# Gated linear attention and two expert layers: column blocks in runs, one scan per step, float32 second products in the first units

## The chip, the cores and the metric

The kernel runs on one core of a Trainium2 chip, as one program. The metric is device time in microseconds (us), as the median of several executions; lower is better. The core has five engines with a queue of instructions each: PE (TensorE; its weight loads are shown apart as PEld), DVE (VectorE), ACT (ScalarE), POOL (GpSimd) and SP (SyncE, which here issues the DMAs).

## The reference

Three stages follow one another on 3072 tokens (4 sequences of 768, width 384 = 8 heads of 48):

```python
f = 1.0 / (1.0 + np.exp(-f_logit))
for t in range(S):
    state = f[:, :, t, :, None] * state + einsum('bhd,bhe->bhde', k[:, :, t], v[:, :, t])
    y[:, :, t] = einsum('bhd,bhde->bhe', q[:, :, t], state)
# x = y as (3072, 384)
x = ((x @ w_a) * (x @ w_b)) @ w_out            # 384 -> 1536 -> 384
p = domain_probs / (domain_probs.sum(-1, keepdims=True) + 1e-09)
for e in range(4):                             # 384 -> 1024 -> 384
    out += p[:, e:e + 1] * (np.maximum(x @ w1[e], 0.0) @ w2[e])
```

The weights of both expert layers and the result are wanted to float32 accuracy. Here the weights of the first layer arrive as 64-bit floats.

## The kernel before

**Phase A** holds the attention and the first expert layer. The attention is cut into 24 steps `s` (6 chunks of 128 time steps for each of the 4 sequences). A step's tiles hold 8 heads as 4 column groups `j` of 128 times, with the two heads of a group in partitions 0 to 47 and 64 to 111. For a step, `a_exp` (L188) computes u = 1 + exp(-f_logit), the exponential on ACT and the addition on DVE (L191). `a_scan` (L194) makes the running product R of u with one DVE scan for each of the four groups (L196); its second operand `cap` is a bound that is broadcast along the row. From step `EARLY` (8) on, a reciprocal for each group follows on DVE (L200). `a_hat` scales k by R (on POOL) and q by 1/R; for the first 8 steps this takes a chain of ACT, POOL and DVE instructions (L217 to L225), for the others fewer (L211 to L215). `a_trans` (L238), `a_scores` (L251) and `a_out` (L286, L294, L303) are the step's matrix products, all in float32; `a_out` also makes the new state, 64 wide, of which 48 columns hold a head (L331, L333), and writes the step's x, split into two parts.

Every product of the expert layers is taken from split operands: a number is rounded to the format float32r (`hi`) and the rest is kept (`lo`), and hi·hi, hi·lo and lo·hi are summed in PSUM, three matmuls of one pass instead of one in float32. `split` (L116) does the first part on ACT (L118) and the rest on POOL or DVE (L119). The work of the first layer is cut into *units* `u`: one block `i` of 512 tokens and one column block `f` of 128 of the 1536 columns (the first four units are 256 tokens wide). A unit takes two first products (`half`, L342, 9 matmuls each), their product `ab` on DVE (L457), the split of `ab` into `hl` and of the block of `w_out` into `wo`, and, one unit later, the second product (`outp`, L354, 9 matmuls). Up to `u` = 19 the `lo` parts are POOL's work, from `LATE` (20) on DVE's. The 64-bit weights are converted by seven instructions each (`to_f32`, L100 to L113), six of them on DVE.

`attn_to` and `conv_to` interleave the steps' operations and the conversions with the units; a scheduler then settles each engine's order. `busy` (L172) fills PE's early gaps with products of a tile of zeros, `junk`.

**Phase B** is the second expert layer: for each expert `e`, token block `n` (6 of 512) and column block `f` (8 of 128), `b1` makes one first product (L490, 9 matmuls of 512 columns), evacuated by ACT (L492) and DVE (L493) into a tile `h`, of which the pool `hp` holds three; `b2` is the second product (L508, 12 matmuls of 384 columns into the banks 4 to 7). The loop at L534 writes them alternately: `b1` of a column block, then `b2` of the one before. The weights of the next expert are loaded and split by `load_e` as tiles come free.

Of the kernel before, what the change touches and what calls it, by code (L numbers as in the profile page):

```python
# [8 lines left out]
F32 = mybir.dt.float32  # L9
F32R = mybir.dt.float32r  # L10
BF16 = mybir.dt.bfloat16
# [29 lines left out]
CA = 2  # L41
FRAC = 0.4
LATE = 20
LIMIT = float(2.0 ** 60)
# [6 lines left out]
def gla_moe_moe_kernel(ctx: ExitStack, tc, qkf, vv, wab, wout, w12, probs, gq, gv, gp, out):  # L51
# [20 lines left out]
    mask = const.tile([128, 128], F32, tag="mask", name="mask")  # L72
    cap = const.tile([128, 1], F32, tag="cap", name="cap")
    nc.vector.memset(cap, 2.0 * LIMIT)
    pr = const.tile([128, NSTEP, NE], F32, tag="pr", name="pr")
    prs = const.tile([128, NSTEP], F32, tag="prs", name="prs")
    flags = const.tile([128, NSTEP, 3], F32, tag="flags", name="flags")
    junk = const.tile([128, 512], BF16, tag="junk", name="junk")
    nc.vector.memset(junk, 0.0)
# [49 lines left out]
    def phase_a(actx):  # L129
# [37 lines left out]
        def busy(n):  # L167

            if n:
                b = bank("o")  # L170
                for _ in range(n):
                    nc.tensor.matmul(b, junk[:, :128], junk, start=True, stop=True)  # L172

# [14 lines left out]
        def a_exp(s):  # L188
            u = T[s]["f"]
            nc.scalar.activation(out=u, in_=u, func=AF.Exp, scale=-1.0)  # L190
            nc.vector.tensor_scalar(out=u, in0=u, scalar1=1.0, scalar2=None, op0=ALU.add)  # L191
            T[s]["R"] = slot("R")

        def a_scan(s, j):  # L194
            u, R = T[s]["f"], T[s]["R"]
            nc.vector.tensor_tensor_scan(  # L196
                out=R[:, j], data0=u[:, j], data1=cap.to_broadcast([128, C]), initial=1.0, op0=ALU.mult, op1=ALU.min
            )
            if s >= EARLY:
                nc.vector.reciprocal(out=u[:, j], in_=R[:, j])  # L200

# [73 lines left out]
        def a_out(s):  # L275
# [14 lines left out]
            if c:  # L290
                for j in range(4):
                    for h in range(2):
                        r = 64 * h
                        nc.tensor.matmul(  # L294
                            yps[r:r + 64, j * C:(j + 1) * C], st[r:r + D, j], q[r:r + D, j],
                            start=False, stop=True, skip_group_check=True,
                        )
            if not last:
                ups = bank("u")
                for j in range(4):  # L300
                    for h in range(2):
                        r = 64 * h
                        nc.tensor.matmul(  # L303
                            ups[r:r + 64, j * 64:(j + 1) * 64], kt[:, j, r:r + 64], v[:, 2 * j + h],
                            start=j == 0, stop=True, skip_group_check=True,
                        )
# [18 lines left out]
            if not last:  # L325
                new = at.tile([128, 4, 64], F32, tag="st", name="st", bufs=B + 1)
                uv = ups[:, :256].rearrange("p (j e) -> p j e", j=4)
                pe = t["pe"].to_broadcast([128, 4, 64])
                sign = 1.0 if s >= EARLY else -1.0
# [17 lines left out]
        def outp(i, o, n, f, fs, w, hl):  # L347
            if (i, fs[0]) not in x2ps:
                x2ps[i, fs[0]] = [bank("o") for _ in range(KC)]
            banks = x2ps[i, fs[0]]  # L350
            for m in range(KC):
                for q, (a, b) in enumerate(((0, 0), (0, 1), (1, 0))):

# [38 lines left out]
        def prep_ops(n):  # L392
            return [lambda: a_exp(n)] + [lambda j=j: a_scan(n, j) for j in range(4)] + [lambda: a_hat(n)]

# [47 lines left out]
        for u, (i, o, n, f, fs) in enumerate(units):  # L442
# [12 lines left out]
            pb = half(i, o, n, f, 1)  # L455
            ab = g.tile([128, n], F32, tag="ab", name="ab")
            nc.vector.tensor_tensor(out=ab, in0=pb, in1=a, op=ALU.mult)  # L457
            hl = g.tile([128, 2, n], F32R, tag="hl", name="hl", bufs=2)
            split(nc.vector if u >= LATE else nc.gpsimd, hl[:, 0], hl[:, 1], ab)
            w = g.tile([128, 2, DM], F32R, tag="wo", name="wo", bufs=2)  # L460
            split(nc.vector if u >= LATE else nc.gpsimd, w[:, 0], w[:, 1], wo_all[:, f])
            attn_to(goal)
# [8 lines left out]
    def phase_b(bctx):  # L471
        xb = bctx.enter_context(tc.tile_pool(name="xb", bufs=NBLK - 1))
        hp = bctx.enter_context(tc.tile_pool(name="hp", bufs=3))
        stg = bctx.enter_context(tc.tile_pool(name="stg", bufs=2))
# [57 lines left out]
        pend = [(0, f) for f in range(3, NF2)] + [(e, f) for e in range(1, NE) for f in range(NF2)]  # L532
        prev = None
        for e, n, f in [(e, n, f) for e in range(NE) for n in range(NBLK) for f in range(NF2)]:  # L534
            h = b1(e, n, f)
            if prev is not None:
                b2(*prev)
            prev = (e, n, f, h)
            if e == 0 and f == 4 and n + 2 < NBLK:
                x2_split(n + 2, xb, "x2", None)  # L540
            if pend and (e, n) == (0, 0):
                load_e(*pend.pop(0))
            elif pend and pend[0][0] == e + 1:

                m = pend[0][1]
                if (n > m and f == 4) if m < 2 else (n == NBLK - 1 and f >= m - 1):
                    load_e(*pend.pop(0))
        b2(*prev)

# [204 lines left out]
```

## Time and profile before

| | us |
|---|---|
| median of 3 executions (1445.41 to 1447.91) | 1446.5 |
| the profiled execution, its own time | 1444.91 |
| span of the profiled execution | 1443.2 |
| PE busy, share of the span | 1397.1, 97% |
| PE weight loads | 1194.9, 83% |
| DVE busy | 601.7, 42% |
| ACT busy | 388.3, 27% |
| POOL busy | 220.8, 15% |

The page gives the whole span; where the two phases lie, and which engine is full in each, is read from the table by windows. Phase A ends at about 632 us. In the trace a row of the timeline gives the start and the length of a group of instructions; matmuls overlap, so the pace of a sequence is read from start to start and not from the length of a row.

### The profile page before, as it was taken

What the parts mean: (1) busy time and instruction counts of PE and PEld (TensorE: products, weight loads), DVE (VectorE), ACT (ScalarE), POOL (GpSimd) and SP (SyncE); (2) the same over time, 40 slices, a digit from 0 to 9 for tenths busy, and PEclk for the clock granted to TensorE, in tenths of its full rate; (3) what the DMA queues carried; (4) which work ended last, traced back from release to release, by engine and by line L of the source; (5) the groups of instructions that cost most, each with busy time, mean ns of one, the idle gap of its engine ahead of it and who ended that gap; (6) DMA issues with size and microseconds to landing.
All of it is one profiled execution on the core that took longest, in us unless ns stands there. A gap on an engine that the chain in (4) does not pass through costs nothing.

```text
span 1443.2 us, 18215 instructions
## 1 busy us (share of the span) xinstructions
PE 1397.1 (97%) x7623; PEld 1194.9 (83%) x7623; DVE 601.7 (42%) x976; ACT 388.3 (27%) x701; POOL 220.8 (15%) x144
## 2 busy tenths in 40 slices
PE   8778899999999999999999999999999999999998
PEld 4556687778878778889999999999999999999997
DVE  7999835884573834532222222222222222222221
ACT  5454423433342323441111211111211112111111
POOL 4456451010010101350000310000300002000000
PEclk9899999999999999999999999999999999999999
DMA  6444201221130100210000110000200001000001
GB/s 247 137 152 130 74 0 31 76 88 34 42 95 1 57 28 11 61 38 0 1 1 0 56 33 1 0 1 1 88 1 0 1 0 44 1 22 23 22 33 36
DMA packets 28170, 60.29 MB, mean 42 GB/s; under 512 B 4016, under 2 KB 9392, under 8 KB 28080
## 3 DMA queue, kind: packets, MB, share of 16 engines
q1 hardware_dynamic: 28080, 59.05, 13.0%
q8 instruction: 62, 1.02, 0.3%
q14 instruction: 28, 0.23, 0.1%
HBM read 51.95 MB, written 4.72 MB: 39 GB/s over the span
## 4 chain that ended last, share of the span: by engine, by line
PE 77%; DVE 1%; ACT 0%; POOL 0%; issue 0%; DVEq 0%; POOLq 0%
PE bank L508 28%; PE bank L490 28%; PE bank L342 13%; PE bank L354 6%; PE bank L286 1%; PE bank L251 1%; PE bank L294 1%; PE bank L303 0%; PE bank L238 0%; DVE hl L119 0%; DVE f L200 0%; DVE acc L518 0%; POOL k L211 0%; DVE ss L267 0%; DVE ab L457 0%
## 5 line engine op out<-in xcount | busy, mean ns | idle before, releaser
L508 PE MATMUL bank<-w,h 128*128 128x384 f32 x2304 | 435.0, 337 | 0.0
L490 PE MATMUL bank<-x,w 128*128 128x512 f32 x1728 | 430.5, 393 | 0.0
L508 PEld LDWEIGHTS bank<-w,h 128*128 128x128 f32 x2304 | 409.7, 188 | 16.9
L490 PEld LDWEIGHTS bank<-x,w 128*128 128x128 f32 x1728 | 321.4, 188 | 58.6
L493 DVE SCALAR_TENSOR_TENSOR h<-bank,h 128x512 fp32r<-128x512 f32 x192 | 132.7, 691 | 541.1 <-ACT h L492 541.1
L342 PE MATMUL bank<-xT,w 128*128 128x512 f32 (+1 forms) x1332 | 322.4, 391 | 4.6 <-DVE ab L457 2.2
L342 PEld LDWEIGHTS bank<-xT,w 128*128 128x128 f32 x1332 | 245.7, 191 | 57.5 <-DVE ab L457 3.1
L492 ACT ACTIVATE h<-bank 128x512 fp32r<-128x512 f32 x192 | 115.0, 599 | 624.9 <-PE bank L490 624.9
L354 PE MATMUL bank<-hl,wo 128*128 128x512 f32 (+1 forms) x666 | 166.3, 392 | 4.7 <-POOL hl L119 3.2
L354 PEld LDWEIGHTS bank<-hl,wo 128*128 128x128 f32 x666 | 122.7, 190 | 32.6 <-POOL hl L119 4.3
L119 POOL TENSOR_TENSOR w<-raw,w 128x768 fp32r<-128x768 f32 x32 | 59.1, 1846 | 579.7 <-ACT w L118 577.7
L457 DVE TENSOR_TENSOR ab<-bank,a 128x512 f32<-128x512 f32 (+1 forms) x74 | 49.7, 671 | 143.2 <-PE bank L342 135.0
L118 ACT CAST hl<-ab 128x512 fp32r<-128x512 f32 (+1 forms) x74 | 45.0, 608 | 102.9 <-DVE ab L457 102.8
L453 ACT COPY a<-bank 128x512 f32<-128x512 f32 (+1 forms) x74 | 42.4, 574 | 95.0 <-PE bank L342 94.8
L518 DVE SCALAR_TENSOR_TENSOR acc<-bank,pr,acc 128x384 f32<-128x384 f32 x72 | 40.9, 609 | 58.9 <-PE bank L508 58.9
L119 DVE TENSOR_TENSOR hl<-ab,hl 128x512 fp32r<-128x512 f32 x54 | 50.6, 937 | 29.4 <-ACT hl L118 29.4
L211 POOL TENSOR_TENSOR k<-k,R 128x512 f32<-128x512 f32 x16 | 21.4, 1335 | 245.9 <-DVE R L196 171.0
L200 DVE RECIPROCAL f<-R 128x128 f32<-128x128 f32 x64 | 58.0, 925 | 0.0
L118 ACT CAST wo<-wo_all 128x384 fp32r<-128x384 f32 x74 | 38.1, 516 | 38.3 <-PE bank L354 37.8
L119 POOL TENSOR_TENSOR hl<-ab,hl 128x512 fp32r<-128x512 f32 (+1 forms) x20 | 34.7, 1737 | 51.2 <-ACT hl L118 51.1
L118 ACT CAST w<-raw 128x768 fp32r<-128x768 f32 x32 | 26.8, 838 | 48.4 <-PE bank L508 34.4
L119 DVE TENSOR_TENSOR wo<-wo_all,wo 128x384 fp32r<-128x384 f32 x54 | 31.9, 590 | 12.9 <-ACT wo L118 12.9
(101 smaller groups left out, 775.4 us busy)
## 6 DMA issues: line engine op xcount, KB each, us to landing
raw<-in_w_dram SPq DMA_DIRECT2D x32, 384.0 KB, 3.1
raw<-in_wab_dram SPq DMA_DIRECT2D x12, 768.0 KB, 4.4
f<-in_qkf_dram SPq DMA_DIRECT2D x20, 256.0 KB, 2.7
k<-in_qkf_dram SPq DMA_DIRECT2D x20, 256.0 KB, 2.7
q<-in_qkf_dram SPq DMA_DIRECT2D x20, 256.0 KB, 3.0
v<-in_v_dram SPq DMA_DIRECT2D x20, 256.0 KB, 3.5
raw<-in_wout_dram SPq DMA_DIRECT2D x6, 768.0 KB, 4.7
out_dram<-acc SPq DMA_DIRECT2D x24, 192.0 KB, 1.9
```

The lines of the kernel that those rows point to most:

```text
L118: nc.scalar.copy(out=hi, in_=x)
L119: engine.tensor_tensor(out=lo, in0=x, in1=hi.bitcast(F32), op=ALU.subtract)
L200: nc.vector.reciprocal(out=u[:, j], in_=R[:, j])
L342: nc.tensor.matmul(p, l, r, start=m == 0, stop=m == len(ops) - 1)
L354: nc.tensor.matmul(banks[m][:, o:o + n], w[:, a, m * 128:(m + 1) * 128], hl[:, b], start=f == fs[0] and q == 0 and o == 0, stop=f == fs[-1 ...
L453: nc.scalar.copy(out=a, in_=pa)
L457: nc.vector.tensor_tensor(out=ab, in0=pb, in1=a, op=ALU.mult)
L490: nc.tensor.matmul(p, l, r, start=i == 0, stop=i == len(ops) - 1)
L492: nc.scalar.activation(out=h[:, 0], in_=p, func=AF.Relu)
L493: nc.vector.scalar_tensor_tensor(out=h[:, 1], in0=p, scalar=0.0, in1=h[:, 0].bitcast(F32), op0=ALU.max, op1=ALU.subtract)
L508: nc.tensor.matmul(src, h[:, b, t * 128:(t + 1) * 128], w2[e, f][:, a], start=f == 0 and q == 0, stop=f == NF2 - 1 and q == 2,)
L518: nc.vector.scalar_tensor_tensor(out=dst, in0=src, scalar=p, in1=dst, op0=ALU.mult, op1=ALU.add)
```

## The change

Four edits, each at its own place:

- In phase B the column blocks are taken in runs: `b1` of all blocks of a run, then `b2` of all blocks of the run before. A run is 4 blocks in the token blocks 1 to 4, 2 blocks in token blocks 0 and 5, and (1, 1, 2, 2, 2) at the very start. The pool `hp` holds 7 tiles instead of 3. `load_e` of the next expert stands behind the `b2` that frees its tile.
- One scan of 512 elements makes all four groups' running products. It starts afresh at each group because `cap` is now a full tile whose first element of each group is set to u itself (a copy of 4 elements on ACT), so that the minimum of product and cap there is u. The addition of 1 moves from DVE to ACT.
- In the first 8 units (`WHOLE`) the second product is taken from unsplit float32 operands: 3 float32 matmuls in place of 9, and no split of `ab` and `w_out`.
- The states are 48 columns wide instead of 64: fewer moving columns in L303, fewer stationary ones in L294, and fewer elements in L331 and L333. The tile `junk` is smaller and is read by broadcast; its matmuls keep their shape.

```diff
+WHOLE = 8
...
-    cap = const.tile([128, 1], F32, tag="cap", name="cap")
+    cap = const.tile([128, 4, C], F32, tag="cap", name="cap")
     nc.vector.memset(cap, 2.0 * LIMIT)
...
             nc.scalar.activation(out=u, in_=u, func=AF.Exp, scale=-1.0)
-            nc.vector.tensor_scalar(out=u, in0=u, scalar1=1.0, scalar2=None, op0=ALU.add)
+            nc.scalar.activation(out=u, in_=u, func=AF.Identity, bias=1.0)
+            nc.scalar.activation(out=cap[:, :, 0:1], in_=u[:, :, 0:1], func=AF.Copy)
             T[s]["R"] = slot("R")
 
-        def a_scan(s, j):
+        def a_scan(s):
+
             u, R = T[s]["f"], T[s]["R"]
+            flat = [x.rearrange("p j c -> p (j c)") for x in (R, u, cap)]
             nc.vector.tensor_tensor_scan(
-                out=R[:, j], data0=u[:, j], data1=cap.to_broadcast([128, C]), initial=1.0, op0=ALU.mult, op1=ALU.min
+                out=flat[0], data0=flat[1], data1=flat[2], initial=1.0, op0=ALU.mult, op1=ALU.min
             )
+
+        def a_inv(s, j):
             if s >= EARLY:
-                nc.vector.reciprocal(out=u[:, j], in_=R[:, j])
+                nc.vector.reciprocal(out=T[s]["f"][:, j], in_=T[s]["R"][:, j])
...
-                            yps[r:r + 64, j * C:(j + 1) * C], st[r:r + D, j], q[r:r + D, j],
+                            yps[r:r + D, j * C:(j + 1) * C], st[r:r + D, j], q[r:r + D, j],
...
-                            ups[r:r + 64, j * 64:(j + 1) * 64], kt[:, j, r:r + 64], v[:, 2 * j + h],
+                            ups[r:r + 64, j * D:(j + 1) * D], kt[:, j, r:r + 64], v[:, 2 * j + h, :D],
...
             for m in range(KC):
+                if w is None:
+                    nc.tensor.matmul(
+                        banks[m][:, o:o + n], wo_all[:, f, m * 128:(m + 1) * 128], hl,
+                        start=f == fs[0] and o == 0, stop=f == fs[-1], skip_group_check=True,
+                    )
+                    continue
...
-            return [lambda: a_exp(n)] + [lambda j=j: a_scan(n, j) for j in range(4)] + [lambda: a_hat(n)]
+            return [lambda: a_exp(n)] + [lambda: a_scan(n)] + [lambda j=j: a_inv(n, j) for j in range(4)] + [lambda: a_hat(n)]
...
+            if u < WHOLE:
+                hl, w = g.tile([128, n], F32, tag="hl", name="hl", bufs=2), None
+                nc.vector.tensor_tensor(out=hl, in0=pb, in1=a, op=ALU.mult)
+            else:
...
-        hp = bctx.enter_context(tc.tile_pool(name="hp", bufs=3))
+        hp = bctx.enter_context(tc.tile_pool(name="hp", bufs=7))
...
+        runs = []
+        for e in range(NE):
+            for n in range(NBLK):
+                sizes = (1, 1, 2, 2, 2) if (e, n) == (0, 0) else (2, 2, 2, 2) if n in (0, NBLK - 1) else (4, 4)
+                f = 0
+                for k in sizes:
+                    runs.append([(e, n, f + i) for i in range(k)])
+                    f += k
+        prev = []
+        for run in runs + [[]]:
+            made = []
+            for e, n, f in run:
+                made.append((e, n, f, b1(e, n, f)))
+                if e == 0 and f == 4 and n + 2 < NBLK:
+                    x2_split(n + 2, xb, "x2", None)
+                if pend and (e, n) == (0, 0):
                     load_e(*pend.pop(0))
-        b2(*prev)
+            for p in prev:
+                b2(*p)
+                e, n, f, _ = p
+                if pend and (e, n) != (0, 0) and pend[0][0] == e + 1:
+
+                    m = pend[0][1]
+                    if (n > m and f == 4) if m < 2 else (n == NBLK - 1 and f >= m - 2):
+                        load_e(*pend.pop(0))
+            prev = made
```

In the order of instructions the change shows at three places.

PE in phase B, expert 0, a token block in the middle (before, L490 is `b1` and L508 `b2`):

```order
L490 MATMUL bank_69<-x_5044,w_5151 128x512 x9
L508 MATMUL bank_71<-w_5122,h 128x384 x3
L508 MATMUL bank_72<-w_5122,h 128x384 x3
L508 MATMUL bank_73<-w_5122,h 128x384 x3
L508 MATMUL bank_74<-w_5122,h 128x384 x3
L490 MATMUL bank_70<-x_5044,w_5185 128x512 x9
```

The same in the change (L507 is `b1`, L525 is `b2`), the beginning of a run:

```order
L507 MATMUL bank_67<-x_4900,w_4936 128x512 x9
L507 MATMUL bank_68<-x_4900,w_4966 128x512 x9
L507 MATMUL bank_69<-x_4900,w_4983 128x512 x9
L507 MATMUL bank_70<-x_4900,w_5017 128x512 x9
L525 MATMUL bank_71<-w_4887,h 128x384 x3
L525 MATMUL bank_72<-w_4887,h 128x384 x3
L525 MATMUL bank_73<-w_4887,h 128x384 x3
L525 MATMUL bank_74<-w_4887,h 128x384 x3
L525 MATMUL bank_71<-w_4892,h 128x384 x3
```

Where before 9 matmuls of 512 columns alternate with 12 of 384, now 36 follow one another and then 48; over phase B the blocks of L490 and L508 go from 191 of each to 64 of each.

POOL in phase A during the first units, before (`hl`, `wo` and `w` are the `lo` parts of L119):

```order
L219 TENSOR_TENSOR k<-k,R 128x512
L119 TENSOR_TENSOR hl<-ab,hl 128x256
L223 TENSOR_TENSOR R<-R,f 128x512
L119 TENSOR_TENSOR wo<-wo_all,wo 128x384 x2
L119 TENSOR_TENSOR hl<-ab,hl 128x256
L119 TENSOR_TENSOR w<-cv,w 128x768
L261 AFFINE_SELECT ss<-ss 128x512
```

And in the change:

```order
L226 TENSOR_TENSOR k<-k,R 128x512
L121 TENSOR_TENSOR w<-cv,w 128x768
L230 TENSOR_TENSOR R<-R,f 128x512
L268 AFFINE_SELECT ss<-ss 128x512
L226 TENSOR_TENSOR k<-k,R 128x512
```

The sixteen splits of the first 8 units (8 `hl`, 8 `wo`) are gone from POOL, and their sixteen casts from ACT.

DVE in phase A, one step's scan, before:

```order
L191 TENSOR_SCALAR f<-f 128x512
L106 SCALAR_TENSOR_TENSOR cv<-raw,cv 128x768
L103 TENSOR_SCALAR cv<-cv 128x768
L109 TENSOR_SCALAR cv<-cv 128x768
L267 TENSOR_TENSOR ss<-bank_73,mask 128x512
L196 SCALAR_TENSOR_TENSOR R<-f,cap 128x128 x4
```

And in the change:

```order
L274 TENSOR_TENSOR ss<-bank_73,mask 128x512
L471 TENSOR_TENSOR hl<-bank_68,a 128x256
L201 SCALAR_TENSOR_TENSOR R<-f,cap 128x512
```

The addition has left DVE and the four scans are one. Up to the product `ab` of the tenth unit DVE has issued 9 additions, 34 scans of 128 and 12 state operations before, and 9 scans of 512 and 12 narrower state operations in the change.

## Rows read from the trace of the kernel before

**Rows 1.** The page: span, busiest engines, the chain that ended last.

```profile
span 1443.2 us, 18215 instructions
...
PE 1397.1 (97%) x7623; PEld 1194.9 (83%) x7623; DVE 601.7 (42%) x976; ACT 388.3 (27%) x701; POOL 220.8 (15%) x144
...
PE 77%; DVE 1%; ACT 0%; POOL 0%; issue 0%; DVEq 0%; POOLq 0%
```

**Rows 2.** Windows: from:to, length, busy PE, PEld, DVE, ACT, POOL, clock, DMA.

```profile
10.00:50.00 40.00, 33.25 (x259) 20.29 (x258) 38.25 (x62) 22.23 (x45) 20.70 (x15) 0.91 0.60 212
50.00:100.00 50.00, 35.58 (x301) 29.16 (x301) 47.39 (x70) 24.24 (x48) 25.28 (x19) 0.86 0.43 140
100.00:154.00 54.00, 44.85 (x269) 35.10 (x265) 52.77 (x66) 21.50 (x37) 32.47 (x18) 0.94 0.39 121
230.00:340.00 110.00, 106.64 (x777) 83.21 (x777) 88.25 (x175) 42.98 (x89) 11.07 (x8) 1.00 0.26 75
632.00:1438.00 806.00, 804.28 (x4035) 728.44 (x4033) 184.16 (x291) 141.06 (x226) 58.74 (x32) 1.00 0.05 16
```

**Rows 3.** Timeline of PE, 632 to 647 us: start, length, instruction, count.

```profile
634.43 0.39 PE L490 MATMUL bank<-x,w 128*128 128x512 f32 x1
636.47 2.27 PE L508 MATMUL bank<-w,h 128*128 128x384 f32 x12
638.57 2.24 PE L490 MATMUL bank<-x,w 128*128 128x512 f32 x9
640.65 2.27 PE L508 MATMUL bank<-w,h 128*128 128x384 f32 x12
641.72 0.51 PE L508 MATMUL bank<-w,h 128*128 128x384 f32 x2
642.76 2.24 PE L490 MATMUL bank<-x,w 128*128 128x512 f32 x9
```

**Rows 4.** Groups of DVE, 10 to 154 us: count, busy us, mean ns, idle before.

```profile
L101 DVE TENSOR_SCALAR cv<-cv 128x768 f32<-128x768 f32 x15 | 15.4, 1043 | 0.0
L109 DVE TENSOR_SCALAR cv<-cv 128x768 uint32<-128x768 uint32 x15 | 11.4, 763 | 0.0
L331 DVE TENSOR_TENSOR st<-bank,st 128x256 f32<-128x256 f32 x4 | 1.7, 413 | 0.0
```

**Rows 5.** Timeline of DVE, single places of the first 50 us.

```profile
10.29 1.37 DVE L196 TENSOR_TENSOR_SCAN R<-qkf,cap 128x128 f32<-128x128 f32 x4
12.10 0.68 DVE L267 TENSOR_TENSOR ss<-bank,mask 128x512 f32<-128x512 f32 x1
29.52 0.55 DVE L109 TENSOR_SCALAR cv<-cv 128x768 uint32<-128x768 uint32 x1
33.25 0.54 DVE L101 TENSOR_SCALAR cv<-cv 128x768 f32<-128x768 f32 x1
47.90 0.41 DVE L191 TENSOR_SCALAR f<-f 128x512 f32<-128x512 f32 x1
```

**Rows 6.** Groups of POOL, 10 to 154 us, the same columns as rows 4.

```profile
L119 POOL TENSOR_TENSOR wo<-wo_all,wo 128x384 fp32r<-128x384 f32 x10 | 14.1, 1421 | 7.4 <-ACT wo L118 7.4
L119 POOL TENSOR_TENSOR hl<-ab,hl 128x512 fp32r<-128x512 f32 x5 | 12.1, 2427 | 9.9 <-ACT hl L118 9.8
L119 POOL TENSOR_TENSOR hl<-ab,hl 128x256 fp32r<-128x256 f32 x4 | 4.0, 1008 | 11.3 <-ACT hl L118 11.3
```

**Rows 7.** Timeline of PE: float32 products of the attention, and what follows each.

```profile
47.27 1.16 PE L251 MATMUL bank<-qkf 48*128 48x128 f32 x16
48.36 0.39 PE L172 MATMUL bank<-junk 128*128 128x512 bf16 x1
...
119.97 0.69 PE L303 MATMUL bank<-v,kt 128*64 128x64 f32 x16
120.59 0.50 PE L342 MATMUL bank<-xT,w 128*128 128x512 f32 x1
```

**Rows 8.** Waits over the whole span: us in total, times, longest.

```profile
ACT j L229 <- POOL k L211: 26.9, 15, 5.2
```

More of the change, by code (lines that the diff above doesn't have):

```diff
@@ L77, in gla_moe_moe_kernel @@
     flags = const.tile([128, NSTEP, 3], F32, tag="flags", name="flags")
-    junk = const.tile([128, 512], BF16, tag="junk", name="junk")
+    junk = const.tile([128, 1, 128], BF16, tag="junk", name="junk")
     nc.vector.memset(junk, 0.0)
@@ L171, in busy @@
                 for _ in range(n):
-                    nc.tensor.matmul(b, junk[:, :128], junk, start=True, stop=True)
+                    nc.tensor.matmul(b, junk[:, 0], junk.to_broadcast([128, 4, 128]), start=True, stop=True)
         def slot(name):
@@ L325, in a_out @@
             if not last:
-                new = at.tile([128, 4, 64], F32, tag="st", name="st", bufs=B + 1)
-                uv = ups[:, :256].rearrange("p (j e) -> p j e", j=4)
-                pe = t["pe"].to_broadcast([128, 4, 64])
+                new = at.tile([128, 4, D], F32, tag="st", name="st", bufs=B + 1)
+                uv = ups[:, :4 * D].rearrange("p (j e) -> p j e", j=4)
+                pe = t["pe"].to_broadcast([128, 4, D])
                 sign = 1.0 if s >= EARLY else -1.0
@@ L455, in phase_a @@
             pb = half(i, o, n, f, 1)
[L456 to L461, printed above, removed]
+            if u < WHOLE:
+                hl, w = g.tile([128, n], F32, tag="hl", name="hl", bufs=2), None
+                nc.vector.tensor_tensor(out=hl, in0=pb, in1=a, op=ALU.mult)
+            else:
+                ab = g.tile([128, n], F32, tag="ab", name="ab")
+                nc.vector.tensor_tensor(out=ab, in0=pb, in1=a, op=ALU.mult)
+                hl = g.tile([128, 2, n], F32R, tag="hl", name="hl", bufs=2)
+                split(nc.vector if u >= LATE else nc.gpsimd, hl[:, 0], hl[:, 1], ab)
+                w = g.tile([128, 2, DM], F32R, tag="wo", name="wo", bufs=2)
+                split(nc.vector if u >= LATE else nc.gpsimd, w[:, 0], w[:, 1], wo_all[:, f])
             attn_to(goal)
@@ L532, in phase_b @@
         pend = [(0, f) for f in range(3, NF2)] + [(e, f) for e in range(1, NE) for f in range(NF2)]
[L533 to L536, printed above, removed]
-                b2(*prev)
[L538 to L546, printed above, removed]
-                    load_e(*pend.pop(0))
-        b2(*prev)
+        runs = []
[14 more added lines that the diff above has]
+                if pend and (e, n) == (0, 0):
+                    load_e(*pend.pop(0))
+            for p in prev:
[6 more added lines that the diff above has]
+            prev = made
     def general(gctx):
```

## The prediction

> **What bounds the kernel now.** I read the page first: PE is busy 97% of the span and holds 77% of the chain that ended last, DVE is at 42% [rows 1]. That average hides two regimes, so the windows come next [rows 2]. From 10 to 154 us DVE is busy 138.4 of 144 us and PE only 113.7: here DVE is the bound, since its queue never runs dry while PE waits for what it makes (and part of PE's work there is `junk`). From 632 us on PE is busy 804.3 of 806 us at full clock and DVE 184.2: the experts are bound by PE alone, and nothing but the pace of the matmuls can change their time. Between 230 and 340 us PE is nearly full (106.6 of 110) with DVE close behind (88.3). So each edit is priced in its own regime: work taken from DVE counts before 154 us, work on PE counts after.
>
> **Runs in the experts.** The number of matmuls stays. The reader is to look at starts [rows 3]. The kernel begins phase B with two `b1` in a row, 18 matmuls of 512 columns, and the tenth starts at 634.43; from there to the next group at 636.47 are nine matmuls in 2.04 us. In every later place nine of them follow twelve of 384 columns, and take 638.57 to 640.65, 2.08 us. The same on the other side: of the twelve of 384, the first six take 640.65 to 641.72, 1.07 us, and the last six 641.72 to 642.76, 1.04 us. So after each change of shape PE runs some 2% slower for some nine matmuls, then settles; no wait stands in these places. An alternation costs 0.04 + 0.03 = 0.07 us. The order of PE shows 191 blocks of each kind before and 64 in the change: 127 × 0.07 = **8.9 us less**. The starts are rounded to hundredths, so the sum lies between 6 and 11 us.
>
> The cover that this needs: a run of four has up to eight `h` alive and the pool has seven, so the fourth evacuation waits for the first `b2` of the run before, and ACT stands meanwhile. Its bank is needed again only three `b1` and up to four `b2` later, some 12 us, against about 1.3 us for both evacuations; next weights are behind it on ACT, and they are used several runs later. I cost this at nothing. The `load_e` of token block 5 now come in pairs behind two `b2`; a tile is then used three runs later, over 20 us. At nothing too.
>
> Here the Trainium skill ("TensorE: Matmul & The Clock Gate", section "Back-to-back issue gap") speaks against the edit: it gives the gap of a warm matmul as its columns divided by 2.4 GHz plus 2.5 ns, whatever came before it. By that the order of shapes is free and the term would be 0 instead of 8.9. The rows show two paces for the same columns, 2.08 and 2.04 us for nine, so I go by them.
>
> **DVE's stretch, 10 to 154 us.** Up to the tenth unit's `ab`, the last point where DVE leads, DVE loses nine additions of 0.41 us [rows 5]: 3.7 us. Thirty-four scans of 128 become nine of 512. Four scans of 128 take 1.37 us [rows 5]. A scan of 512 is in no row: from below it costs what another two-input instruction of 512 elements costs, 0.68 us [rows 5], from above the 1.37 of the four. A two-input instruction takes 0.41 us for 256 elements and 0.68 for 512 [rows 4, 5], that is 1.05 ns an element and 0.14 fixed; one scan of 128 at about 0.41 has then twice that per element, so 0.14 + 512 × 2.1 ns = 1.2 us. I take this, 0.15 us less than four, nine times: 1.4 us (ends 0 and 6). Twelve state operations shrink by a quarter of 0.27 us: 0.8 us. Together **6 us**.
>
> The larger part is indirect. L101 takes 1043 ns on average in this stretch and 0.54 us where nothing disturbs it, L109 763 ns and 0.55 [rows 4, 5]; these two groups alone are stretched by 15 × 0.50 + 15 × 0.21 = 10.7 us. They share the time with POOL, which is busy 78 us of these 144 [rows 2]. Taking the other 170 or so instructions as stretched by a third to a half as much each (0.12 to 0.18 us), DVE loses some 30 to 40 us to it. The change takes from POOL four `hl` of 256, four of 512 and eight `wo`: 4 × 1.0 + 4 × 2.4 + 8 × 1.4 = 25 us [rows 6], a third of its work. A third of 30 to 40 is 10 to 13 us; at the low end the collisions only move to other pairs and nothing is won, at the high end the removed splits are the worst ones, 20 us. I take **10 us**, nearer to the proportional value.
>
> Against this stands PE. Sixteen float32 instructions (a float32 matmul is two) of 128 columns take 47.27 to 48.36, two halves of the array side by side: 0.136 us for a pair; of 64 columns 119.97 to 120.59, 0.078 us [rows 7]. The slope, 0.92 ns a column, makes a 512-column instruction 0.47 us, and a second product of 3 × 2 of them 2.8 us instead of the nine at 2.04: +0.8 us for four units, half of it for the four narrow ones, 4.5 us (ends: -2 if the halves of a pair in fact follow one another and an instruction alone takes 0.068 us per 128 columns, +7 at four times 0.136). PE has 30 us to spare in the stretch, but not everywhere; I count 4 us as seen. ACT loses sixteen casts and gains for each step an activation of 512 and one of 4 elements; it is half idle (67.9 of 144), so I count nothing. The first units' PE no longer waits for POOL's `hl`; that is inside the 10 us. Sum of the stretch: 6 + 10 - 4 = **12 us less** (ends 2 and 22).
>
> **The rest of phase A.** The fifteen later steps take about 0.41 + 0.15 + 0.13 us less of DVE each, 10 us in all, where DVE is second: I take 1.5 us of the 3.4 that PE idles between 230 and 340. L303 loses 16 of 64 columns: by the slope 0.015 us a pair, 0.12 a step; eleven such steps where PE leads, 1.3 us. Together **3 us** (ends 0 and 6).
>
> **The sum** is 8.9 + 12 + 3 = 24 us. The profiled execution took 1444.9 us of its own time (span 1443.2), so 1421; the median of the runs shown is 1446.5, 1.6 higher. I give **1422 us**.
>
> **Rivals.** *The runs bring nothing* (7%): the 2% belong to something other than the change of shape. For it: no wait is seen, so the cause is inferred from one place, the 18 matmuls. Against: the settled pace shows in both shapes. Then 12 + 3 = 15 us less: 1431. The rule of the Trainium skill quoted above would end here; no run here decides on it yet.
>
> *PE takes over early* (15%): DVE gets free but PE, with float32 products and the attention's steps between the units, is full from about 100 us on, and the collisions with POOL only move. For it: PE is busy 44.9 of the 54 us from 100 to 154 [rows 2], and float32 adds to it. Then the stretch gives 2 us: 1432.
>
> *DVE and POOL come apart more fully* (9%): the high ends, 20 + 6 less in the stretch and 5 later: 1409.
>
> *The wait of `cap`* (4%, slower): there is one `cap`, so the copy of step s + 1 on ACT must wait until the scan of step s has been read on DVE, and behind it on ACT stand the evacuations of the units and the casts. Today ACT waits fifteen times for the chain behind a scan, 1.8 us each [rows 8]. If each of the 16 steps without the long chain made ACT stop once more like this with PE behind it, 29 us would be added and the time would be 1450; it turns slower from 1.5 us a step (24 / 16). Against: the order places the copy a step behind the previous scan, and ACT is half idle.
>
> That the order does not do what it says is excluded by the 64 blocks.
>
> **Numbers.** The forecast has 65%. The range reaches from the high ends, 1409, to rivals one and two with their ends, 1436; outside it lie half of the third rival, the fourth and the tails, 2 in 10. A measurement can tell 0.2%, 2.9 us, from no change. Slower by more than that needs the fourth rival: 0.04. Within it: only if the runs and the stretch both fail, 0.04. Faster: 0.92.
>
> **What would show it.** Right: in phase B nine matmuls of a later place in a run take 2.04 us and six of 384 columns 1.04, and the stretch from the first `b1` to the end is some 9 us shorter; the first `b1` starts about 15 us earlier than 632; L101 and L109 fall clearly on average; one scan of 512 takes about 1.2 us. Wrong: alternation gone but 2.08 us still in the middle of a run; the first `b1` not earlier than 628; the copy to `cap` waiting on DVE more than 1 us a step; PE waiting in phase B for an `h` or a weight.

## The result and the profile after

| | before | after |
|---|---|---|
| median of 4 executions, us | 1446.6 (1445.41 to 1447.91) | 1422.93 (1422.56 to 1423.61) |
| ratio, 95% interval | 1 | 0.9837 (0.982 to 0.9854) |
| profiled execution, own time | 1444.91 | 1423.61 |
| span | 1443.2 | 1421.8 |
| start of the first `b1` (end of phase A) | 632.26 | 619.66 |
| from there to the end | 810.9 | 802.1 |

The forecast was 1422.0, the range 1409 to 1436. Of the 21.4 us that the span lost, 8.8 lie in phase B (forecast 8.9) and 12.6 in phase A (forecast 15).

The page of the changed kernel. The chain that ended last is empty in it, so phase B is read from starts.

```profile
span 1421.8 us, 18079 instructions
...
PE 1382.4 (97%) x7599; PEld 1185.1 (83%) x7599; DVE 582.2 (41%) x880; ACT 394.2 (28%) x733; POOL 192.3 (14%) x128
```

Windows of the changed kernel, the columns and stretches of [rows 2]; the last one begins at its own first `b1`.

```profile
10.00:50.00 40.00, 32.28 (x264) 19.88 (x262) 35.69 (x56) 24.59 (x51) 16.29 (x12) 0.96 0.56 200
50.00:100.00 50.00, 40.00 (x344) 32.56 (x344) 47.10 (x65) 25.61 (x53) 21.11 (x15) 0.90 0.47 161
100.00:154.00 54.00, 45.96 (x223) 31.79 (x222) 49.84 (x60) 20.86 (x39) 24.47 (x15) 1.00 0.39 129
230.00:340.00 110.00, 108.22 (x793) 85.91 (x792) 79.61 (x140) 46.58 (x101) 10.30 (x8) 1.00 0.26 75
620.00:1416.00 796.00, 795.22 (x4032) 724.90 (x4030) 185.66 (x289) 140.79 (x226) 58.67 (x32) 1.00 0.05 16
```

From 10 to 154 us POOL is busy 61.9 us where it was 78.5, DVE 132.6 of 144 where it was 138.4: DVE still leads. The granted clock of PE (the third number from the right, as a share of 2.4 GHz) also differs: 0.96, 0.90 and 1.00 in the first three windows, where it was 0.91, 0.86 and 0.94. It has two levels here, 1.0 and 0.5 (1.2 GHz). In the early windows, in which PE also waits (busy 40.0 of the 50 us with 0.90), it is at the lower one for a part; in the last two, with PE busy 98% and more, it stays at 1.00. In phase B PE idles less than 1 us of 796.

Timeline of PE in phase B, changed kernel (start, length, instruction, count); it answers to [rows 3].

```profile
648.82 8.36 PE L507 MATMUL bank<-x,w 128*128 128x512 f32 x36
657.02 4.35 PE L525 MATMUL bank<-w,h 128*128 128x384 f32 x24
661.20 8.36 PE L507 MATMUL bank<-x,w 128*128 128x512 f32 x36
669.40 8.51 PE L525 MATMUL bank<-w,h 128*128 128x384 f32 x48
677.75 0.63 PE L507 MATMUL bank<-x,w 128*128 128x512 f32 x2
```

Read start to start: 36 matmuls of `b1` take 657.02 - 648.82 = 8.20 us, as one nine at 2.08 and three at 2.04 would. 24 of `b2` take 4.18 (by 1.07 and three sixes at 1.04 it would be 4.19), 48 take 8.35 (1.07 and seven at 1.04). Matmul by matmul the trace shows the same: over phase B the first nine of a run of `b1` take 2.081 us, and every later one 0.2267 (2.040 for nine). The slow start comes once a run, the rest is settled.

Groups of DVE from 10 to 154 us, changed kernel (L103 and L111 were L101 and L109 in [rows 4]), and the new scan, by line over the whole span (shortest/median/longest ns, first and last start).

```profile
L111 DVE TENSOR_SCALAR cv<-cv 128x768 uint32<-128x768 uint32 x15 | 12.8, 852 | 0.0
L103 DVE TENSOR_SCALAR cv<-cv 128x768 f32<-128x768 f32 x15 | 9.9, 659 | 1.0 <-ACT cv L102 1.0
...
L201 DVE TENSOR_TENSOR_SCAN R<-f,cap x6: 1206/1215/2829, 50.0 to 165.0; 128x512 f32<-128x512 f32 x6
L201 DVE TENSOR_TENSOR_SCAN R<-qkf,cap x4: 1206/1214/1225, 5.2 to 30.7; 128x512 f32<-128x512 f32 x4
```

The undisturbed scan of 512 takes 1.21 us, the estimate was 1.2. L103 fell from 1043 to 659 ns, but L111 rose from 763 to 852: not both fell, as the prediction wanted. The longest scan took 2829 ns, so the stretching goes on.

What stretches them can be seen in one place. Timeline of DVE and POOL in the changed kernel:

```profile
123.35 5.25 POOL L121 TENSOR_TENSOR wo<-wo_all,wo 128x384 fp32r<-128x384 f32 x2 [5.58 <-ACT wo L120]
...
124.46 0.55 DVE L105 TENSOR_SCALAR cv<-cv 128x768 uint32<-128x768 uint32 x1
...
128.07 0.95 DVE L111 TENSOR_SCALAR cv<-cv 128x768 uint32<-128x768 uint32 x1
128.56 2.16 POOL L121 TENSOR_TENSOR w<-cv,w 128x768 fp32r<-128x768 f32 x1
128.94 2.20 DVE L103 TENSOR_SCALAR cv<-cv 128x768 f32<-128x768 f32 x1
131.06 0.95 DVE L112 SCALAR_TENSOR_TENSOR cv<-raw,cv 128x768 f32<-128x768 uint32 x1
...
134.13 0.55 DVE L103 TENSOR_SCALAR cv<-cv 128x768 f32<-128x768 f32 x1
134.28 2.10 POOL L121 TENSOR_TENSOR w<-cv,w 128x768 fp32r<-128x768 f32 x1 [3.56 <-ACT w L120]
134.60 2.20 DVE L111 TENSOR_SCALAR cv<-cv 128x768 uint32<-128x768 uint32 x1
```

L103, 0.55 us by itself, takes 2.20 when it starts behind POOL's subtraction: it ends at 131.14, 0.42 after POOL (130.72). L111 does the same at 134.60, and at 128.07 behind the end of POOL's pair (128.60): each ends 0.42 us after POOL. The DVE instruction is not slowed by a share; it stands until POOL's has ended, and then runs. It also goes the other way: of the two subtractions of POOL at 123.35, 1.0 us each where nothing disturbs them, one takes 4.3 us, while DVE's own instructions run on at 0.55 and 0.95. The Trainium skill ("SBUF — State Buffer", section "Who interferes with whom") says that a DVE instruction which uses the ports shared with GpSimd contends for them as for an exclusive lock: whoever issues first holds the pair for the whole instruction, and the other is fully blocked. These rows agree.

### The profile page after: what moved, and what is told of

Same layout as the page of the kernel before. It is cut to its first block, busy times and chain, and to the rows that moved or that the text cites. A ratio compares the mean times of both kernels' runs of the same rounds, so it can differ in the third digit from the quotient of the medians.

```text
span 1421.8 us, 18079 instructions
## 1 busy us (share of the span) xinstructions
PE 1382.4 (97%) x7599; PEld 1185.1 (83%) x7599; DVE 582.2 (41%) x880; ACT 394.2 (28%) x733; POOL 192.3 (14%) x128
## 4 chain that ended last, share of the span: by engine, by line
## 5 line engine op out<-in xcount | busy, mean ns | idle before, releaser
L525 PE MATMUL bank<-w,h 128*128 128x384 f32 x2304 | 411.3, 335 | 0.0
L525 PEld LDWEIGHTS bank<-w,h 128*128 128x128 f32 x2304 | 402.8, 188 | 5.0
L507 PE MATMUL bank<-x,w 128*128 128x512 f32 x1728 | 404.8, 390 | 0.0
L507 PEld LDWEIGHTS bank<-x,w 128*128 128x128 f32 x1728 | 323.3, 188 | 65.2
L367 PE MATMUL bank<-hl,wo 128*128 128x512 f32 x594 | 149.0, 393 | 2.1 <-DVE hl L121 1.1
L367 PEld LDWEIGHTS bank<-hl,wo 128*128 128x128 f32 x594 | 110.0, 188 | 27.4 <-DVE hl L121 1.8
L474 DVE TENSOR_TENSOR ab<-bank,a 128x512 f32<-128x512 f32 x66 | 45.1, 683 | 144.7 <-PE bank L349 140.4
L120 ACT CAST hl<-ab 128x512 fp32r<-128x512 f32 x66 | 40.8, 618 | 86.4 <-DVE ab L474 86.4
L120 ACT CAST wo<-wo_all 128x384 fp32r<-128x384 f32 x66 | 33.9, 515 | 28.4 <-PE bank L367 27.6
L258 PE MATMUL bank<-q,k 48*128 48x128 f32 x320 | 25.8, 296 | 7.2 <-DVE q L231 5.8
```

The source lines that it names most:

```text
L120: nc.scalar.copy(out=hi, in_=x)
L367: nc.tensor.matmul(banks[m][:, o:o + n], w[:, a, m * 128:(m + 1) * 128], hl[:, b], start=f == fs[0] and q == 0 and o == 0, stop=f == fs[-1 ...
L507: nc.tensor.matmul(p, l, r, start=i == 0, stop=i == len(ops) - 1)
L525: nc.tensor.matmul(src, h[:, b, t * 128:(t + 1) * 128], w2[e, f][:, a], start=f == 0 and q == 0, stop=f == NF2 - 1 and q == 2,)
```

## The experiments

All times by stage, from each kernel's trace: when the product of unit `u` = 11 (`ab`) starts on DVE, when the first `b1` starts, the stretch between, and the rest. The last column is DVE's instructions of the conversions (tile `cv`) from 10 to 170 us: their count, and their busy time divided by it. Medians and ratios are of their own sets; before's median in them was 1445.56 to 1446.17.

| kernel | median | ratio (95%) | u11 | first `b1` | between | phase B | `cv`, ns |
|---|---|---|---|---|---|---|---|
| before | 1446.6 | 1 | 166.5 | 632.3 | 465.7 | 810.9 | x90, 986 |
| after | 1422.93 | 0.9837 (0.982 to 0.9854) | 156.8 | 619.7 | 462.9 | 802.1 | x97, 868 |
| e1 runs alone | 1436.47 | 0.9938 (0.9924 to 0.9951) | 167.0 | 632.8 | 465.8 | 801.7 | x90, 982 |
| e2 after, no runs | 1431.92 | 0.9905 (0.9889 to 0.992) | 154.7 | 617.6 | 462.9 | 810.4 | |
| e3 scan and states alone | 1442.2 | 0.997 (0.9958 to 0.9982) | 167.0 | 629.4 | 462.4 | 810.6 | x91, 995 |
| e4 float32 alone | 1431.16 | 0.9898 (0.9883 to 0.9913) | 152.5 | 618.2 | 465.7 | 810.8 | x101, 841 |
| e5 states alone | 1445.51 | 0.9999 (0.9989 to 1.0008) | 165.2 | 632.4 | 467.2 | 811.1 | |
| e6 after, no float32 | 1426.39 | 0.9867 (0.9852 to 0.9882) | 160.1 | 622.6 | 462.5 | 802.0 | x97, 936 |
| e7 `b2` in 512 columns | 1425.7 | 0.9864 (0.9849 to 0.9879) | 167.3 | 633.0 | 465.7 | 790.6 | |
| e8 after, POOL's load back | 1431.98 | 0.9904 (0.9889 to 0.9919) | 165.6 | 628.6 | 463.0 | 801.9 | x93, 923 |
| e9 `junk` alone | 1449.15 | 1.0019 (1.001 to 1.0028) | 171.5 | 637.3 | 465.8 | 810.7 | x90, 971 |
| e11 float32 and runs | 1422.47 | 0.9837 (0.9823 to 0.985) | 152.7 | 618.5 | 465.8 | 802.0 | x100, 847 |
| e12 after, early scans old | 1425.43 | 0.9858 (0.984 to 0.9876) | 160.0 | 622.4 | 462.4 | 801.5 | x97, 839 |
| e13 float32 for 12 units | 1419.05 | 0.9814 (0.98 to 0.9829) | 152.7 | 615.5 | 462.8 | 801.9 | x99, 860 |

The same traces tell where DVE's time up to u11 goes. Every kernel's DVE does the 90 conversion instructions of this stretch before u11. In the next table "alone" counts each of DVE's instructions from 10 us to u11 with the length that one in twenty of its kind, over all kernels, stays at or below, "stretched" is what their lengths have beyond that, and "idle" is the time in which none runs. An instruction starts about 0.07 us before the end of the one in front, so the columns sum to more than u11. The last column is PE's granted clock from 10 us to u11.

| kernel | u11 | alone | stretched | idle | clock |
|---|---|---|---|---|---|
| before | 166.5 | 118.2 | 43.2 | 10.0 | 0.90 |
| after | 156.8 | 111.9 | 32.9 | 14.4 | 0.95 |
| e3 | 167.0 | 111.9 | 43.7 | 13.6 | 0.87 |
| e4 | 152.5 | 118.6 | 30.8 | 8.5 | 0.98 |
| e6 | 160.1 | 112.6 | 39.4 | 10.6 | 0.91 |
| e8 | 165.6 | 112.6 | 39.9 | 15.4 | 0.91 |
| e9 | 171.5 | 118.6 | 48.0 | 10.1 | 0.88 |
| e13 | 152.7 | 111.9 | 27.3 | 15.5 | 0.92 |

Of the 43.2 us stretched before, 41.2 lie in the 116 instructions that overlap one of POOL's; of the 32.9 after, 30.8.

### Phase B: e1, e2, e7

**e1** puts the loop in runs, with `bufs=7` in `hp`, into the kernel before; **e2** puts the old loop into the changed kernel.

> The kernel before with the runs of column blocks in the experts alone. Theory (the pace settles: nine 512-column matmuls behind a change of shape take 2.08 us, the next nine 2.04): 1446.6 - 8.8 = 1437.8 us, all of it behind the first b1, whose start stays at 632 us within 1 us. Rival (the runs bring nothing, the 8.8 us come from phase A ending otherwise): 1446.6 us. A second rival (the runs need the earlier end of phase A, for instance because h or a weight arrives late): between the two, with waits of TensorE in phase B.

> The changed kernel with the old alternation in the experts, a first and a second product in turn. Theory (the two halves of the change add up): 1422.9 + 8.8 = 1431.7 us, first b1 at 619.7 us as in the changed kernel. Rival (runs bring nothing): 1422.9 us.

e1 takes 9.2 us off phase B, with phase A where it was; e2 gives 8.3 back. Either way the runs are worth 9 us (medians: 9.5 and 9.0), wherever phase A ends. The rival that they bring nothing is out.

**e7** asks what the 2% hang on, in the kernel before:

```diff
-            for t in range(B):
-                src = banks[n][t][:, :DM]
+            for m in range(KC):
...
-                        src, h[:, b, t * 128:(t + 1) * 128], w2[e, f][:, a],
+                        banks[n][m], w2[e, f][:, a, m * 128:(m + 1) * 128], h[:, b],
```

> The kernel before with the second product of the experts turned round: w2's blocks of 128 columns are the stationary operand and h the moving one, so that a pair of first and second product is 18 matmuls of 512 columns where it was 9 of 512 and 12 of 384, the same 9216 columns. It leaves out the layout of the result: the sums stand transposed and are stored as if they did not. Theory (the slow first nine matmuls are the price of the change of column count): no slow matmuls at the switch, 18 x 0.2265 = 4.08 us per pair where it was 4.187, some 0.11 us over about 190 pairs: 1425 to 1427 us. Rival one (the price is that of the switch between two products, of their banks or operands): the 2.08 us per nine stays at both switches, 4.16 us per pair, 1441 to 1443 us. Rival two (512 columns cost more than 384 by column): slower than 1446.6 us.

Timeline of PE in e7 (L507 is `b2` there):

```profile
649.46 2.20 PE L507 MATMUL bank<-h,w 128*128 128x512 f32 x9
651.50 2.20 PE L490 MATMUL bank<-x,w 128*128 128x512 f32 x9
653.54 2.20 PE L507 MATMUL bank<-h,w 128*128 128x512 f32 x9
655.58 2.20 PE L490 MATMUL bank<-x,w 128*128 128x512 f32 x9
```

Two products, their operands and their banks still alternate every nine matmuls, and each nine takes 2.04 us. So the slow start belongs to the change of column count, 384 to 512 or back, and not to the change of product. Phase B is 20.3 us shorter, 11.1 more than with runs: 64 changes of width are left in e1 at 0.07, and twelve settled matmuls of 384 take 2.08 us where nine of 512 take 2.04, an estimate of 4.5 + 7.7 = 12.2. A kernel that uses this would have to turn the result round; that was not tried. The formula that the prediction takes from the Trainium skill ("TensorE: Matmul & The Clock Gate", section "Back-to-back issue gap") is given there for an isolated matmul, and the section says that it over-counts at 512 columns in a stream. For nine of them it gives 1.94 us; the stream here takes 2.04 settled and 2.08 behind a change, 5% more, and the formula has no term for what came before.

### Phase A: which edit, e3 to e6

**e4** and **e6** move the float32 products: e4 has them alone, e6 sets `WHOLE = 0` in the changed kernel. **e3** has scan, ACT's addition and 48-wide states alone; **e5** only the states (L294, L303, L331, L333).

> The kernel before with the second product of the first eight units in float32 alone; scans, additions and states as before. Theory (most of the 12.6 us by which phase A shrank comes from GpSimd standing still in the stretch from 10 to 154 us while VectorE works): first b1 6 to 9 us earlier, 1438 to 1441 us. Rival one (the direct VectorE work is what counts, TensorE only pays for float32): first b1 0 to 4 us later, 1446.6 to 1450.6 us. Rival two (the parts only bring the time together): 0 to 2 us earlier, 1445 to 1446.6 us.

> The changed kernel with no unit's second product in float32: GpSimd splits hl and wo for the first eight units again, TensorE multiplies in three fp32r passes. Theory (GpSimd standing still is most of the gain): first b1 6 to 9 us later than in the changed kernel, 1429 to 1432 us. Rival one (direct VectorE work counts): 0 to 4 us earlier, 1419 to 1423 us. Rival two (sharing only moves): within 2 us of 1422.9 us.

> The kernel before with one restarted scan per step, the addition of 1 on ScalarE and the 48-wide states (the wider cap needs the memory that the narrower states leave), without the float32 products and without the runs. Theory (the direct VectorE work of these parts is 6 us up to 154 us by the rows of before, half of it or less on the path): first b1 3 to 6 us earlier, 1440.6 to 1443.6 us. Rival (GpSimd's share is all that counts, VectorE has slack): within 1 us of 1446.6 us.

> The kernel before with the 48-wide states alone. Theory (VectorE's state operations shrink by a quarter of their elements, 0.8 us up to 154 us, and TensorE's state matmuls by a quarter of their columns): 0 to 2 us earlier, 1444.6 to 1446.6 us. Rival (state work on GpSimd and VectorE counts for more than its length): 3 us or more earlier.

e4 overshoots the theory, 6 to 9 us: 14.1 us off phase A, all of it before u11. Its windows:

```profile
10.00:50.00 40.00, 31.31 (x253) 19.04 (x258) 37.95 (x66) 22.27 (x43) 17.10 (x12) 0.96 0.62 223
50.00:100.00 50.00, 38.41 (x350) 30.77 (x351) 47.64 (x82) 25.22 (x49) 21.37 (x15) 0.97 0.49 163
100.00:154.00 54.00, 48.16 (x247) 34.32 (x247) 49.27 (x68) 20.16 (x36) 24.94 (x14) 1.00 0.29 97
```

DVE is nearly as full as before (134.9 of 144 us, where it was 138.4 [rows 2]), but it gets 101 conversion instructions done by 170 us where it was 90: they are stretched by 12.4 us less. e3 meets its theory in the time, and not in the place. It moves u11 by nothing (167.0 against 166.5) and takes 3.3 us off the stretch behind u11. DVE does have 6.3 us less to do alone, and is stretched as much as before (43.7), but it idles 3.6 us longer: it waits 3.7 us for ACT where it was 0.5, 8.9 for PE where it was 6.7, and 1.7 less for POOL. Waits of DVE in e3, 10 us to u11:

```profile
DVE xT L320 <- ACT xT L319: 1.8, 4, 0.9
...
DVE qkf L227 <- ACT qkf L223: 1.4, 1, 1.4
DVE ss L272 <- PE bank L256: 1.3, 2, 1.1
```

e5 measures as no change. e6 fell between: the float32 products are worth 14 us in the kernel before and only 3 in the changed one (5.0 against e2, which has the changed kernel's order in phase A), and the rest of the change, worth nothing before u11 in e3, is worth 6.4 us there in e6. Up to u11 the parts do not add.

### The order by itself: e9

e3 and e6 differ in phase A only in the tile `junk` (and in the branch that `WHOLE = 0` never takes), and stand 6.8 us apart at the first `b1`. e9 makes that edit alone:

```diff
-    junk = const.tile([128, 512], BF16, tag="junk", name="junk")
+    junk = const.tile([128, 1, 128], BF16, tag="junk", name="junk")
...
-                    nc.tensor.matmul(b, junk[:, :128], junk, start=True, stop=True)
+                    nc.tensor.matmul(b, junk[:, 0], junk.to_broadcast([128, 4, 128]), start=True, stop=True)
```

> The kernel before with one edit: the tile junk of the filling matmuls, 512 columns wide, becomes 128 columns that are read four times over. No work is added or taken away, but the order in which the engines of the attention and feed-forward part get their instructions shifts with it (on GpSimd and VectorE some dozens of places). It is the control for the two kernels with and without this edit whose first b1 stood 6.8 us apart. Theory (the order by itself is worth several us in the stretch up to 167 us): first b1 moves by 2 us or more from 632.3 us, to 1438 to 1444 us or to over 1448 us. Rival (the order is worth nothing, the 6.8 us come from something else): 1445 to 1447 us.

5.0 us later at the first `b1`, in both u11 and the end, and 3.2 by the medians. The work is the same; the scheduler settles DVE's, ACT's and POOL's order anew, and other pairs meet: DVE's instructions are stretched by 48.0 us where it was 43.2. Differences of several us in this stretch need no explanation by work.

### POOL with the order held: e8

```diff
+                nc.gpsimd.tensor_tensor(out=hh[:, 1], in0=hl, in1=a, op=ALU.subtract)
+                dw = g.tile([128, 2, DM], F32, tag="wo", name="dw", bufs=2)
+                nc.gpsimd.tensor_tensor(out=dw[:, 1], in0=wo_all[:, f], in1=wo_all[:, f], op=ALU.subtract)
```

> The changed kernel with two subtractions on GpSimd put back in each of the first eight units, of the shapes that the float32 products removed, into tiles that nothing reads; ScalarE's copies and TensorE's three passes stay away. It computes the same. Theory (VectorE's additions and multiplications stretch while GpSimd runs): gives back 4 to 8 us, 1427 to 1431 us, and the mean of VectorE's 512-column multiply in front of the scan rises from 0.66 us towards 1.04 us. Rival (the gain is that TensorE does not wait for hl and wo any more): within 1 us of 1422.9 us.

Here DVE, ACT and PE have, row for row, the order of the changed kernel; POOL alone has 16 instructions more. Groups of POOL and of DVE in e8, 10 to 154 us:

```profile
L475 POOL TENSOR_TENSOR dw<-wo_all 128x384 f32<-128x384 f32 x8 | 8.6, 1090 | 9.4 <-DVE wo_all L115 9.4
L473 POOL TENSOR_TENSOR hl<-hl,a 128x512 f32<-128x512 f32 x4 | 7.1, 1776 | 4.2 <-DVE hl L472 4.2
...
L473 POOL TENSOR_TENSOR hl<-hl,a 128x256 f32<-128x256 f32 x4 | 5.0, 1252 | 4.8 <-DVE hl L472 4.8
...
L111 DVE TENSOR_SCALAR cv<-cv 128x768 uint32<-128x768 uint32 x15 | 15.9, 1059 | 0.0
L103 DVE TENSOR_SCALAR cv<-cv 128x768 f32<-128x768 f32 x15 | 12.4, 824 | 0.7 <-ACT cv L102 0.7
```

20.7 us of POOL, whose results nobody reads, put the first `b1` 8.9 us later and the median 9.05, a little more than the 4 to 8 of the theory. PE does not wait for them, so the rival that the gain was PE's wait for `hl` and `wo` falls. DVE is stretched by 7.0 us more and idles 1.0 longer. L111 rises from 852 to 1059 ns and L103 from 659 to 824: 3.1 and 2.5 us of the 8.9 in these two groups. Not every group rises: L108, not among these lines, falls from 1369 to 1178 ns. (I had called L103 the multiply in front of the scan; it is the first conversion.)

### What joins, and a faster version: e11, e12, e13

**e11** is e4 with e1's loop. **e12** keeps the four scans of 128 and DVE's addition for the first eight steps of the changed kernel (`if s < OLD`). **e13** is the changed kernel with `WHOLE = 12`.

> The kernel before with the float32 second products and the runs; scans, additions, states as before. Theory (inside the stretch the float32 products are the whole gain, and the runs add to it): 1431.2 - 9.2 = 1422 us, as fast as the changed kernel within 1.5 us, first b1 at 618 us. Rival (the scan part carries 3 us or more of the changed kernel's time): 1425 us or more.

> The changed kernel in which the first eight steps scan and add as before (four scans of 128 columns, the addition on VectorE) and the later ones as in the change. It joins the two halves that were fastest apart: the float32 products with the old scans up to u11 (152.5 us), and the new scans behind it (462.6 us where the old ones took 465.7). Theory: first b1 at 152.5 + 462.7 = 615.2 us, and 1418 us in all. Rival (the order of the instructions, which the edit moves, decides and not the scan's form): anywhere from 1416 to 1424 us, with u11 not at 152 to 153 us. Second rival (the 3 us behind u11 hang on something of the first steps): 1421 to 1422 us.

> The changed kernel with the second product in float32 for the first twelve units instead of eight, so that GpSimd splits neither hl nor wo before u12. Theory (GpSimd's share of the stretch is the price): four more units free of 3.4 to 3.8 us of GpSimd each, a few of them inside the stretch in which VectorE is late, 1 to 3 us earlier at u11, 1420 to 1422 us. Rival (from u8 on TensorE is what is late, and float32 costs it about half a us per unit): 1423.5 to 1426 us. Second rival (the order of the instructions moves again and covers both): outside 1419 to 1426 us.

e11 is as fast as the whole change: 1422.47, as its theory had it. Scan, addition and states, with the order that comes with them, bring nothing to the total beside the other two edits; with them the stretch behind u11 is 3 us shorter and the one before it 2 to 4 longer. e12 was to keep the one and avoid the other, and missed: u11 stands at 160.0, so the old scans alone do not bring e4's u11 back. The rival of the order fits by u11, though its range ended at 1424 and the median is 1425.43. e13 beats both kernels, 3.9 us faster than the change (1416.83 to 1421.55 against 1422.56 to 1423.61), a little below the range its theory gave; u11 is 4.1 us earlier, where the theory had 1 to 3. Its window from 100 to 154 us:

```profile
100.00:154.00 54.00, 51.46 (x226) 35.27 (x225) 43.10 (x61) 17.63 (x32) 13.67 (x7) 0.94 0.35 116
```

From 100 to 154 us POOL falls from 24.5 to 13.7, and PE, at 51.5 of 54 where it had 46.0, is now what is full there, part of it at the lower clock (0.94). That the lever ends about here is my reading; no run takes more units. How much of the 3.9 us is the order's, this run cannot tell.

## Why the prediction was right

**Runs, 8.9 us: right, cause and size.** 8.8 in the changed kernel, 9.2 in e1. That PE "runs some 2% slower for some nine matmuls, then settles" was inferred from one place; the rows of the changed kernel show it for whole runs, and e7 shows that it hangs on the column count. The pool of seven and `load_e` cost nothing: in phase B no wait for an `h` or a weight shows, and PE is busy 795.2 of 796 us.

**DVE's stretch, 12 us: near, but not as a sum of the edits.** Measured at u11: 9.7 us in the changed kernel's profile, 11.8 in e2's, whose order in phase A is the same. In the changed kernel the terms come out near one by one: DVE's own lengths fall by 6.3 us ("Together **6 us**"), the stretching by 10.3 ("I take **10 us**"), and 4.4 us of idle time stand against them, where the prediction had 4 for PE. In time the 6.3 are less, since 31 instructions fewer also overlap 2.5 us less, and of the longer idle time only 1.4 us are waits for PE; 2.3 are waits for ACT, for which the prediction counted nothing because it is half idle.

The edits by themselves do not have these prices. "Together **6 us**" assumes that what is taken from DVE's queue comes off the time: e3 takes it all, and DVE only waits longer, for ACT and PE. The float32 products alone bring 14.0 us at u11 (e4), where 10 - 4 = 6 was forecast for them. And e9 changes the stretching by 4.8 us with no change of work. So the mechanism is right (DVE's instructions stand behind POOL's, and fewer of POOL's shorten them), and that the terms fit so closely at this order is partly luck. The proportional estimate that a removed microsecond of POOL saves 10/25 = 0.4 on DVE was good: e8 measures 8.9/20.7 = 0.43 with the order held. Of PE's "4 us as seen" the work is there: a float32 instruction of 512 columns takes 0.43 us, six of them 2.6 where the nine took 2.04, some 3 us for the eight units. What of it was paid cannot be told apart.

**The rest of phase A, 3 us: right in size, in part for another cause.** 465.7 us from u11 to the first `b1` became 462.9. I had put it down to 1.5 us of PE's idle time and to 1.3 for L303's columns. Waits of PE from u11 to the first `b1`, before (L238 is `a_trans`):

```profile
PE bank L238 <- POOL k L211: 3.0, 6, 0.7
PE bank L354 <- DVE hl L119: 1.1, 1, 1.1
...
```

and in the changed kernel:

```profile
PE bank L293 <- DVE ss L274: 1.5, 2, 1.2
PE bank L367 <- DVE hl L121: 1.1, 1, 1.1
PE bank L258 <- DVE q L221: 0.9, 2, 0.5
...
```

Before, PE waited six times for POOL's scaling of k, which waits for R. With R from one scan these 3.0 us are gone, but others have come for them: all waits together are 5.5 us before and 5.2 after. What shrank is the time of the matmuls without waits, start to start: L303 from 9.1 to 8.3 us, the attention's L286 and L294 together from 33.7 to 32.8, and the first layer's products of 512 columns from 395.1 to 393.7. The first is the cause that I had named, at 0.8 of its 1.3 us. For the last I have no shown cause; in this stretch PE's stream changes from one line to another 264 times where it was 281. The states alone (e5) show L303's 0.8 as well. That e5's stretch is 467.2 all the same comes from 1.3 us more of waits, and from 3.4 us at the lower clock (185.6 to 189.0 us) that the kernel before does not have there.

**The rivals.** *The wait of `cap`* did not come. The copy's line in the changed kernel, with what ACT waited for before it (nothing) and who waited for it:

```profile
L194 ACT ACTIVATE cap<-f x20: 195/210/214, 47.3 to 480.3; 128x4 f32<-128x4 f32 x20
...
its engine sat idle before it (us, times) until:
who waited for it (us, times):
  DVE R L201: 3.7, 1
  PEld bank L293: 3.5, 1
  PE bank L293: 3.0, 1
```

In 24 copies ACT never stood until a scan had read `cap`, where the rival needed 1.5 us a step. The other way round a scan waited once for the copy, 3.7 us, and PE once, 3.0. ACT's wait for the chain behind the scan did grow [rows 8], to this in the changed kernel,

```profile
ACT j L236 <- POOL k L218: 64.2, 16, 6.3
```

and cost nothing that shows in the stage times. *PE takes over early* did not come either: PE is busy 46.0 of the 54 us from 100 to 154; it comes only with e13. For the last 5.7 us before u11, though, DVE waits for PE (3.8 before). *DVE and POOL come apart more fully* was the direction of e4 and e13, short of its 1409.

**What stays open** is what the scan and ACT's addition are worth before u11 at an equal order: e3, e6 and e12 each moved the order as well. PE's clock is open too, since it moved with the order: up to u11 it was 0.87 in e3, 0.90 before and 0.98 in e4, and no run holds it. Two pairs speak against it as the main cause: e1 has the order of the kernel before and 0.92, with u11 at 167.0, and e13 has 0.92 with u11 at 152.7, as early as e4.

## What to carry to other kernels

Where PE alone is the bound, count the changes of column count in the stream of matmuls, not only the columns: grouping matmuls of one width gave 0.07 us for each pair of changes removed, at no cost but buffers. Where DVE is the bound and POOL runs beside it, take work from POOL before DVE: a microsecond of POOL cost 0.4 here at an equal order, while 6 us of DVE's own work, taken off alone in e3, gave nothing up to u11. And where a scheduler sets the order, run one edit that changes the order and no work before explaining a few us.

## What was not expected of the hardware

- Matmuls of 512 columns take 2.04 us per nine when the matmuls in front have 512 columns, whatever product they belong to, and 2.08 behind 384 columns.
- A DVE instruction of 0.55 us that starts behind a POOL subtraction takes 2.20, until 0.42 us after POOL's end; and a POOL subtraction of 1.0 us took 4.3 while DVE's instructions ran on.
- The same order of phase A ended 2.1 us apart in two profiled executions (first `b1` at 619.7 in the changed kernel and 617.6 in e2), and an edit that only moves the order was worth 5.0.
